# Sixty-four weight columns instead of 128 for one of five products, and another order of two

## The chip, the cores and the metric

One core of a Trainium2 chip runs the whole program. The metric is the device time of one execution in microseconds. The kernel before was timed in 3 runs.

## What is computed

The reference takes `x` of 4 x 4096 tokens with 192 channels through three layers; 16,384 tokens in all.

```
w   = softmax(weight, axis=-1)              # 8 heads x 7 taps
x1  = causal convolution of x over 7 tokens, 24 channels per head
x2  = (sigmoid(x1 @ w_gate) * (x1 @ w_val)) @ w_out      # 192 -> 1536 -> 192
out = relu(x2 @ w_in2)**2 @ w_out2                       # 192 -> 2048 -> 192
```

## The kernel before, in words

**Split numbers.** Matrix operands go to TensorE as float32r. So that a product keeps enough digits, each operand is split into a high part (the number cast to float32r) and a low part (the rest). A product is then the sum of three: high weight by high activation, high weight by low activation, low weight by high activation. The weights are split once at the start (`convert`, L126); of the hidden activations `gh` is the high part (`high`, L540, on ScalarE) and `gl` the low one (`low`, L546, on VectorE).

**Stages.** The tokens are cut into 32 tiles of 512. For each tile there is a phase of stage one (the gated layer, 12 units of 128 hidden channels) and a phase of stage two (the squared layer, 8 units of 2 x 128 hidden channels). From the sixth tile on the phases alternate: stage one of tile t, stage two of tile t - 5.

**Rows and columns.** A unit first computes its hidden channels (`rows`, L509): 9 steps, each of two matmuls. The first works on partitions 0 to 63 of the array (`HALVES[0]`), the second on 64 to 127, and each adds to a bank of its own. Then ScalarE and VectorE make `gh` and `gl` of a hidden block of 128 channels by 512 tokens (`activate`, L550). Later `cols` (L561) multiplies each block by the output weights. The 192 output channels go to two banks for each partition half: `accA` holds channels 0 to 127, `accB` channels 128 to 191. The weights for `accB` are 128 columns wide, `wb`: 64 with the high part of channels 128 to 191 and, right behind them, 64 with their low part. So one matmul with `gh` yields the high-by-high product in partitions 0 to 63 and the low-by-high product in 64 to 127. At the end of a phase `fold` (L599) adds the two halves of the array, and the upper 64 partitions of `accB` to the lower ones. A block thus takes five steps in `cols`, each again of two matmuls (L593): three for `accA` (`wa` by `gh`, `wa` by `gl`, `wl` by `gh`) and two for `accB` (`wb` by `gh`, `wb` by `gl`). A unit of stage one has one block, a unit of stage two has two.

**Order.** The program writes the order of every engine out by hand. The loop at L847 issues the rows of a unit, its activations, and then the columns of units before it (`pending`, L861 to L866); loads, convolution and stores are put between them (`side`). All matmuls of a matrix operand bring a weight load of their own, which the trace shows as LDWEIGHTS on PEld. The first matmul on a bank in a phase starts the sum anew (`start=first`), the last of a phase closes it. In the last unit of all, the order is sorted so that `accB` is finished first, and `accA` is summed over all 128 partitions in one matmul (L590).

In the first tiles the convolution runs on TensorE too, in float32 with all 128 rows (L399); later it runs on VectorE.

Of the kernel before, what the change touches and what calls it, by code (L numbers as in the profile page):

```python
# [17 lines left out]
HB = 64  # L18
# [7 lines left out]
def kernel(  # L26
# [86 lines left out]
    def weights2(u):  # L113
        if u not in w2:
            w2[u] = cp.tile([P, NW2], F32R, tag=f"u{u}", name="w2")
        return w2[u][:, 0 : 2 * NR], w2[u][:, 2 * NR :].rearrange("p (b n) -> p b n", b=2)
# [357 lines left out]
    def prep_x(t, a_on_array=False, b_on_array=False):  # L474


        p, i = divmod(t, 2)
        j = p % TPB
        sa, a = convolve("A", i, lambda: xin.pop(t), j, a_on_array)
        b = []  # L480
        if i == 0:
            pairs[p], b = convolve("B", 0, lambda: xin.pop(("B", p)), j, b_on_array)

        def over():
            done(sa)
            if i == 1:
                done(pairs.pop(p))

        return a, b, part_ops(t, x1, "x1", lambda: sa["cv"], lambda: pairs[p]["cv"], over)
# [71 lines left out]
    def cols(u):  # L561

        key = (u.kind, u.t)
        if u.f == 0:
            acc[key] = [[banks.take(f"acc{nm}") for nm in "AB"] for _ in HALVES]
        sums = acc[key]
        order = []
        for i, v in enumerate(u.hidden):  # L570
            if u.kind == 1:
                w, lo = w1[:, u.f, NR:], N1 + HB
            else:
                w, lo = weights2(u.f)[1][:, i, :], NO + HB
            wa, wb, wl = w[:, 0:P], w[:, P : 2 * P], w[:, lo : lo + P]
            first = u.f == 0 and i == 0
            order += [
                (0, wa, v.gh, first), (0, wa, v.gl, False), (0, wl, v.gh, False),
                (1, wb, v.gh, first), (1, wb, v.gl, False),
            ]  # L580
        final = u is units[-1]
        if final:

            order.sort(key=lambda step: -step[0])
        ends = {step[0]: k for k, step in enumerate(order)} if u.last else {}
        if u is units[-2]:
            shut = max(k for k, step in enumerate(order) if step[0] == 0)
        for k, (b, wt, m, first) in enumerate(order):
            if final and b == 0:
                nc.tensor.matmul(sums[0][0][1], wt, m, start=False, stop=ends[b] == k)  # L590
                continue
            for h, half in enumerate(HALVES):
                nc.tensor.matmul(  # L593
                    sums[h][b][1], wt[half], m[half], start=first,
                    stop=ends.get(b) == k or u is units[-2] and (h, b, k) == (1, 0, shut),
                )
        return u.last
# [115 lines left out]
    with tc.manual_schedule():  # L713
# [73 lines left out]
        for t in range(2, NTILE):  # L787
            at = where[1, t, 0]
            before = starts[starts.index(at) - 1]
            a, b, parting = prep_x(t)  # L790
# [56 lines left out]
        for e, u in enumerate(units):  # L847
            rows(u)
            if e < NU1:
                convert_and_activate(e, u)  # L850
            else:
                activate(u)
            for o in stores:
                o()
            stores = []
            k = e - max(s for s in starts if s <= e)

            if e >= NU1 and k == 0:
                for v in u.hidden:
                    low(v)  # L860
            due = len(pending) if k == 0 else 0 if k == 1 else len(pending) - 1  # L861
            for _ in range(due):
                v = pending.popleft()
                if cols(v):
                    stores += (evac1 if v.kind == 1 else evac2)(v.t)
            pending.append(u)  # L866
            for o in side[e]:
                o()
            if e >= NU1 and k:
                for v in u.hidden:  # L870
                    low(v)
        while pending:
            v = pending.popleft()
            if cols(v):
                for o in evac2(v.t):
                    o()
# [39 lines left out]
```

## Time and profile before

| | |
|---|---|
| median of 3 runs | 2363.5 us (2363.48 to 2364.02) |
| span of the profiled execution | 2362.0 us |
| its own time, from first to last instruction | that span; what lies around it is not in the trace |
| TensorE, matmuls | 2347.9 us busy, 20,514 of them |
| TensorE, weight loads | 2301.1 us busy, as many |
| VectorE | 1687.0 us busy (71%) |
| ScalarE | 1314.3 us busy (56%) |
| mean granted clock of TensorE | 1.000 |

PE is the matmul side of TensorE, PEld its weight loads, DVE is VectorE, ACT is ScalarE, SP the engine that starts most DMAs. "Busy" counts the time in which at least one instruction of the engine runs; matmuls overlap, so that the sum of their durations is far larger than the busy time. A row of the timeline gives start, duration, engine, line, operation, output and inputs, shape and count; a number in brackets is the idle time before it and what ended it. "64*128" in a matmul's row is rows by columns of the array that it uses.

### The profile page before, as it was taken

What the parts mean: (1) busy time and instruction counts of PE and PEld (TensorE: products, weight loads), DVE (VectorE), ACT (ScalarE), POOL (GpSimd) and SP (SyncE); (2) the same over time, 40 slices, a digit from 0 to 9 for tenths busy, and PEclk for the clock granted to TensorE, in tenths of its full rate; (3) what the DMA queues carried; (4) which work ended last, traced back from release to release, by engine and by line L of the source; (5) the groups of instructions that cost most, each with busy time, mean ns of one, the idle gap of its engine ahead of it and who ended that gap; (6) DMA issues with size and microseconds to landing.
All of it is one profiled execution on the core that took longest, in us unless ns stands there. A gap on an engine that the chain in (4) does not pass through costs nothing.

```text
span 2362.0 us, 49286 instructions
## 1 busy us (share of the span) xinstructions
PE 2347.9 (99%) x20514; PEld 2301.1 (97%) x20514; DVE 1687.0 (71%) x2679; ACT 1314.3 (56%) x2261; POOL 45.4 (2%) x98
## 2 busy tenths in 40 slices
PE   8999999999999999999999999999999999999998
PEld 5789999999999999999999999999999999999998
DVE  8787866677776776767767677676676766666776
ACT  7555655555555555545555455555555554555665
POOL 1000000000000000000000000000000000000000
PEclk9999999999999999999999999999999999999999
DMA  7123111201212111121011111111111111101111
GB/s 180 32 55 77 46 31 38 43 22 32 44 26 44 33 23 41 26 44 39 21 37 35 35 39 21 37 39 30 39 39 25 34 30 39 35 21 28 42 28 28
DMA packets 226320, 91.87 MB, mean 39 GB/s; under 512 B 202328, under 2 KB 213728, under 8 KB 226096
## 3 DMA queue, kind: packets, MB, share of 16 engines
q1 hardware_dynamic: 224608, 87.93, 17.4%
q8 instruction: 160, 2.62, 0.5%
q0 software_dynamic: 288, 0.59, 0.1%
q14 instruction: 64, 0.52, 0.1%
q10 hardware_dynamic: 1200, 0.20, 0.0%
HBM read 26.03 MB, written 12.58 MB: 16 GB/s over the span
## 4 chain that ended last, share of the span: by engine, by line
PE 82%; issue 16%; DVE 1%; ACT 1%; DMA 0%; SPq 0%; POOL 0%; POOLq 0%; DVEq 0%; ACTq 0%
PE accA L593 21%; PE ph L521 17%; PE pg L521 16%; PE pv L521 14%; PE accB L593 14%; DVE cvA L390 0%; ACT s L534 0%; DMA xiB<-in_x_dram 0%; DVE s L538 0%; ACT pair L152 0%; DMA x<-x 0%; SPq L332 0%; ACT pair L149 0%; POOL xiB L332 0%; DVE pair L174 0%
## 5 line engine op out<-in xcount | busy, mean ns | idle before, releaser
L521 PE MATMUL pg<-x,w 64*128 64x512 f32 x3456 | 842.2, 387 | 4.6 <-ACT w L181 3.6
L521 PE MATMUL pv<-x,w 64*128 64x512 f32 x3456 | 841.7, 387 | 1.0 <-DMA x<-x 0.7
L593 PE MATMUL accA<-gh,w 64*128 64x512 f32 x3576 | 842.1, 386 | 0.0
L543 ACT CAST gh<-s 128x512 fp32r<-128x512 f32 x896 | 556.8, 623 | 432.9 <-DVE s L538 426.3
L548 DVE TENSOR_TENSOR gl<-s,gh 128x512 fp32r<-128x512 f32 x896 | 599.5, 687 | 97.2 <-ACT gh L543 77.2
L521 PEld LDWEIGHTS pg<-x,w 64*128 64x128 f32 x3456 | 635.1, 184 | 18.3 <-ACT w L181 8.0
L521 PEld LDWEIGHTS pv<-x,w 64*128 64x128 f32 x3456 | 634.9, 184 | 11.8 <-DMA x<-x 1.0
L521 PE MATMUL ph<-x,w 64*128 64x512 f32 x4608 | 581.1, 386 | 0.0
L521 PEld LDWEIGHTS ph<-x,w 64*128 64x128 f32 x4608 | 535.8, 184 | 0.0
L593 PEld LDWEIGHTS accA<-gh,w 64*128 64x128 f32 x3576 | 512.7, 184 | 6.0 <-issue 2.3
L538 DVE TENSOR_TENSOR s<-pv,s 128x512 f32<-128x512 f32 x384 | 264.5, 689 | 284.2 <-ACT s L534 284.0
L538 DVE TENSOR_TENSOR s<-s 128x512 f32<-128x512 f32 x512 | 330.1, 686 | 175.9 <-ACT s L534 175.7
L593 PE MATMUL accB<-gh,w 64*128 64x512 f32 x1792 | 438.8, 386 | 0.0
L593 PE MATMUL accB<-gl,w 64*128 64x512 f32 x1792 | 438.7, 386 | 0.0
L593 PE MATMUL accA<-gl,w 64*128 64x512 f32 x1788 | 438.1, 386 | 0.0
L534 ACT ACTIVATE s<-ph 128x512 f32<-128x512 f32 x512 | 280.2, 594 | 213.4 <-PE ph L521 205.0
L534 ACT ACTIVATE s<-pg 128x512 f32<-128x512 f32 x384 | 229.1, 597 | 261.7 <-PE pg L521 202.5
L593 PEld LDWEIGHTS accB<-gh,w 64*128 64x128 f32 x1792 | 256.8, 184 | 1.9
L593 PEld LDWEIGHTS accB<-gl,w 64*128 64x128 f32 x1792 | 256.8, 184 | 1.9
L593 PEld LDWEIGHTS accA<-gl,w 64*128 64x128 f32 x1788 | 256.0, 184 | 2.0 <-DVE gl L548 0.2
L390 DVE SCALAR_TENSOR_TENSOR cvA<-xTA,cw,cvA 128x512 f32<-128x512 f32 x186 | 137.4, 739 | 0.5
L609 ACT COPY ca<-accA 128x512 f32<-128x512 f32 x64 | 37.4, 585 | 64.6 <-PE accA L593 64.6
(87 smaller groups left out, 774.4 us busy)
## 6 DMA issues: line engine op xcount, KB each, us to landing
x<-x SPq DMA_DIRECT2D x191, 256.0 KB, 3.8
out_dram<-oA SPq DMA_DIRECT2D x126, 64.0 KB, 1.9
xiA<-in_x_dram SPq DMA_DIRECT2D x124, 64.0 KB, 2.8
raw<-in_moe_w_out_dram SPq DMA_DIRECT2D x28, 192.0 KB, 3.6
out_dram<-oB SPq DMA_DIRECT2D x63, 64.0 KB, 1.9
xiB<-in_x_dram SPq DMA_DIRECT2D x60, 64.0 KB, 2.4
raw<-in_moe_w_in_dram SPq DMA_DIRECT2D x16, 192.0 KB, 3.4
raw<-in_moe_w_gate_dram SPq DMA_DIRECT2D x12, 192.0 KB, 4.0
```

The lines of the kernel that those rows point to most:

```text
L390: nc.vector.scalar_tensor_tensor(out=st["cv"], in0=st["x"][:, k : k + NT], scalar=cw[:, i, k : k + 1], in1=st["cv"], op0=ALU.mult, op1=ALU ...
L521: nc.tensor.matmul(u.banks[h][1], w[half, o + c * P : o + (c + 1) * P], xs[1][half, place[n] + p, :], start=(i == 0), stop=(i == len(steps ...
L534: nc.scalar.activation(s, u.banks[i][1], AF.Sigmoid if u.kind == 1 else AF.Relu)
L538: nc.vector.tensor_tensor(s, u.banks[1][1] if u.kind == 1 else s, s, op=ALU.mult)
L543: nc.scalar.copy(v.gh, s)
L548: nc.vector.tensor_tensor(v.gl, v.s, v.gh.bitcast(F32), op=ALU.subtract)
L593: nc.tensor.matmul(sums[h][b][1], wt[half], m[half], start=first, stop=ends.get(b) == k or u is units[-2] and (h, b, k) == (1, 0, shut),)
L609: nc.scalar.copy(ca, a1[1])
```

## The change

For the product of `wb` with `gl`, only the 64 columns with the high parts are loaded, and the output is the first 64 partitions of the bank. In every block but the first of a phase this product is issued ahead of the one with `gh`. What partitions 64 to 127 received from it, the product of the low weights with the low activations, is not computed any more. `HB` is 64.

```diff
@@ -576,8 +576,9 @@
             first = u.f == 0 and i == 0
             order += [
                 (0, wa, v.gh, first), (0, wa, v.gl, False), (0, wl, v.gh, False),
-                (1, wb, v.gh, first), (1, wb, v.gl, False),
             ]
+            upper = [(1, wb, v.gh, first), (1, wb[:, 0:HB], v.gl, False)]
+            order += upper if first else upper[::-1]
         final = u is units[-1]
         if final:
 
@@ -591,7 +592,7 @@
                 continue
             for h, half in enumerate(HALVES):
                 nc.tensor.matmul(
-                    sums[h][b][1], wt[half], m[half], start=first,
+                    sums[h][b][1][0 : wt.shape[1]], wt[half], m[half], start=first,
                     stop=ends.get(b) == k or u is units[-2] and (h, b, k) == (1, 0, shut),
                 )
         return u.last
```

## Rows read from the trace of the kernel before

**Rows 1.** The page's head: span, and busy time by engine.

```profile
span 2362.0 us, 49286 instructions
PE 2347.9 (99%) x20514; PEld 2301.1 (97%) x20514; DVE 1687.0 (71%) x2679; ACT 1314.3 (56%) x2261; POOL 45.4 (2%) x98
```

**Rows 2.** Stretches of time: length, busy time by engine, granted clock, DMA.

```profile
400.00:800.00 400.00, 400.00 (x3533) 400.00 (x3531) 282.13 (x436) 219.09 (x378) 7.68 (x16) 1.00 0.16 33
```

**Rows 3.** Chain that ended last: start, length, piece.

```profile
845.02 4.08 PE ph L521 x36
917.55 4.08 PE ph L521 x36
```

**Rows 4.** Instructions grouped by line and shape, whole span.

```profile
L593 PE MATMUL accB<-gh,w 64*128 64x512 f32 x1792 | 438.8, 386 | 0.0
L593 PE MATMUL accB<-gl,w 64*128 64x512 f32 x1792 | 438.7, 386 | 0.0
...
L593 PEld LDWEIGHTS accB<-gl,w 64*128 64x128 f32 x1792 | 256.8, 184 | 1.9
```

**Rows 5.** Timeline from 163.2 us, where a load came late.

```profile
163.32 0.58 PE L593 MATMUL accA<-gh,w 64*128 64x512 f32 x2
...
163.69 0.19 PEld L593 LDWEIGHTS accA<-gl,w 64*128 64x128 f32 x2 [0.21 <-DVE gl L548]
163.69 0.50 PE L593 MATMUL accA<-gl,w 64*128 64x512 f32 x2
163.80 0.19 PEld L593 LDWEIGHTS accA<-gh,w 64*128 64x128 f32 x2
164.03 0.40 PE L593 MATMUL accA<-gh,w 64*128 64x512 f32 x2
```

**Rows 6.** Timeline from 1003.1 us, the steady stretch.

```profile
1003.20 0.49 PE L593 MATMUL accB<-gh,w 64*128 64x512 f32 x2
1003.20 0.29 PEld L593 LDWEIGHTS accB<-gl,w 64*128 64x128 f32 x2
1003.42 0.49 PE L593 MATMUL accB<-gl,w 64*128 64x512 f32 x2
```

**Rows 7.** Timeline of PEld from 11.8 us: loads of the float32 products.

```profile
11.84 0.19 PEld L399 LDWEIGHTS cv<-xTB,diag 128*128 128x128 f32 x1 [0.24 <-issue]
12.27 0.19 PEld L399 LDWEIGHTS cv<-xTB,diag 128*128 128x128 f32 x1 [0.24 <-issue]
...
14.85 0.19 PEld L399 LDWEIGHTS cv<-xTB,diag 128*128 128x128 f32 x1 [0.24 <-issue]
```

**Rows 8.** Timeline from 19.6 us: 64 rows of the array, 128, 64 again.

```profile
19.73 0.39 PE L521 MATMUL pv<-x,w 64*128 64x512 f32 x1
...
20.05 0.30 PEld L399 LDWEIGHTS cv<-xTA,diag 128*128 128x128 f32 x2 [0.36 <-issue]
20.05 2.84 PE L399 MATMUL cv<-xTA,diag 128*128 128x512 f32 x6
...
21.88 0.19 PEld L399 LDWEIGHTS cv<-xTA,diag 128*128 128x128 f32 x1 [0.24 <-issue]
...
22.82 0.18 PEld L521 LDWEIGHTS pg<-x,w 64*128 64x128 f32 x1 [0.76 <-issue]
...
22.93 0.19 PEld L521 LDWEIGHTS pg<-x,w 64*128 64x128 f32 x1
```

**Rows 9.** Waits of PEld: who waited for whom, us in total, times, longest.

```profile
PEld accA L593 <- DVE gl L548: 0.2, 1, 0.2
```

**Rows 10.** Timeline from 30.2 us, after a pause of TensorE.

```profile
30.62 0.39 PE L593 MATMUL accA<-gl,w 64*128 64x512 f32 x2
...
32.24 0.18 PEld L521 LDWEIGHTS pg<-x,w 64*128 64x128 f32 x1
32.24 0.18 PEld L521 LDWEIGHTS pv<-x,w 64*128 64x128 f32 x1
...
32.46 0.39 PE L521 MATMUL pg<-x,w 64*128 64x512 f32 x1
32.47 0.39 PE L521 MATMUL pv<-x,w 64*128 64x512 f32 x1
```

## The prediction

> **What bounds the kernel now.** I read the page's head first: a span of 2362.0 us in which TensorE has a product running 99% of the time and a weight load 97% [rows 1]; VectorE and ScalarE are far from that. The stretches by time say that it is steady: from 400 us on there is no gap on TensorE at all, and the granted clock is 1.00 of 2.4 GHz [rows 2]. The chain shows the period: the 36 matmuls of the stage-two rows begin at 845.02 and again at 917.55 us, 72.53 us later [rows 3]. In between lie one phase of stage one and one of stage two, which by the code issue 12 x (9 + 5) + 8 x (9 + 10) = 320 steps, a step being the two matmuls of the two partition halves. So one step takes 72.53/320 = 0.2267 us, and 32 x 320 = 10,240 steps take 2321 us of the 2362. Any gain or loss of this change has to come out of the length of a step.
>
> A step can be long for two reasons, and the busy shares (99% and 97%) do not part them: its loads, or the passage of its 512 columns. The rows by shape give 184 ns to a load, whatever the tile, and 386 ns to a matmul [rows 4]; each half's loads and matmuls therefore overlap their neighbours, and a mean duration is not a cost. What parts them is a place where a load came late. At 163.69 us the loads for `accA<-gl` had waited for VectorE; their matmuls are recorded at the same moment, but run 0.50 us in place of 0.39, and the next load, which everywhere follows the start of the matmul before it, comes at 163.80 [rows 5]. So a load needs about 0.11 us before its product can pass. The following products come at 164.03, which is 0.23 after 163.80: the ordinary step, though their loads ran beside it. In the steady state the load for a product starts when the product before it does (1003.20 both) and that product comes at 1003.42 [rows 6]. A load of 0.11 us has 0.227 us to be ready in: some 0.11 us of slack on every step. **The step is the passage of the columns, and the loads lie under it.** The rows of the float32 products point the same way: their loads, 0.19 us long, stand 0.43 us apart with 0.24 idle before each [rows 7], so there too the matmul sets the pace.
>
> **The change, part by part.**
>
> 1. *The short load.* There are 384 + 2 x 256 = 896 hidden blocks, each with one step `accB<-gl`: 1792 loads and 1792 matmuls [rows 4]. Their loads go from 128 to 64 columns. The matmul still passes 512 columns, so its own time stays. A load that shrinks by half of its 0.11 us takes 0.055 us off something with 0.11 us of slack already. Cover: the passage of the product before it, 0.227 us; without that cover the gain would be 896 x 0.055 = 49 us. Taken: 0. Bounds: below, nothing lost by the load itself, as it reads less; above, what lies between a step and the bare passage of 512 columns. The nearest rows for that are the float32 products: from 11.84 to 14.85 seven of them take 3.01 us, 0.430 each [rows 7], and half of that, an estimate that takes such a product as two passes, is 0.215 us; 512 columns at one in each cycle of 2.4 GHz are 0.2133. So a step could lose 0.0117 us by the first and 0.0134 by the second; I take the second as the bound, and 896 x 0.0134 = 12.0 us.
>
> 2. *The narrower output.* The matmul writes partitions 0 to 63 of `accB` and leaves out 64 to 127. It has no row of its own in the trace: every matmul there has 128 weight columns. If the array takes it as it takes the others, 0. If not, it needs another division of the array, and the trace has the price of such a change, since the float32 products use all 128 rows and their neighbours 64. Going over: the last 64-row matmul starts at 19.73, the second float32 load, which marks the first float32 passage, at 20.05 + 0.30 - 0.19 = 20.16 us: 0.43 where a step takes 0.23, so 0.20 us lost. Coming back: the last float32 load at 21.88, so its passage at 21.88 + 0.43 = 22.31; the next 64-row passage at 22.93: 0.62 where 0.43 would do, so 0.19 us lost [rows 8]. Twice per block, 896 x 0.39 = 349 us. I take 0, because rows of the array are shared out as before (both halves of 64) and only columns would be, which no row here shows to matter.
>
> The Trainium skill speaks on both sides of this. "TensorEngine Tiling (Array Packing)", Key Properties, says that a change of tiling mode drains the engine, and lists 64x64 as a mode apart from 64x128; [rows 8] agree that a change of mode costs, about 0.2 us each. "PSUM — Partial Sum Buffer" of the Trainium skill, The four PSUM rules, says that float32r matmuls force the mask of all column groups; no run here shows that. By the first the sum would be 2712 us, by the second nothing changes.
>
> 3. *The order.* `gl` now comes ahead of `gh` on `accB`, except in the first block of a phase. Its matmuls would wait for `gl`, but `accA<-gl` stands three steps earlier in the same block and waits for the same tile: over the whole run PE's loads wait 0.2 us for `gl`, once [rows 9]. So no new wait, and nothing moves past a queue: the order of ScalarE, VectorE, POOL and SP's DMAs is untouched. The last product of a phase is still one with all 128 partitions, so the reading of `accB` starts where it did. Cost 0.
>
> 4. *The low-by-low products* that partitions 64 to 127 received are gone. They shared their columns' passage with the others, so no step goes away: 10,240 before and after. Cost 0.
>
> 5. *The last unit* keeps its order by bank; its two `accB<-gl` steps are short ones. Cost 0.
>
> Sum: 0 against the profiled span of 2362.0 us. The median of the runs, 2363.5, is 1.5 us above that span, which lies around it; so 2363.5 us.
>
> **The rivals.**
>
> *A: the loads do space the steps* by way of the remainder above the bare passage, 0.0134 us a step. For it: PEld is busy 97%, and a step is 0.2267 us and not 0.2133, a remainder that I cannot account for. Against it: the slack of 0.11 us in [rows 5], and that the step does not feel when the loads come: it is 0.23 with the two halves' loads at the same moment (32.24 to 32.47 [rows 10]) as with 0.11 between them, where two loads of 0.18 take 0.29 together [rows 6]. [...] If the remainder shrinks by half on the 896 steps, 896 x 0.0067 = 6.0 us: 2357.5; if all goes, 2351.5. Chance 0.23.
>
> *B: the array changes its division* for the 64-column product and back, at 0.39 us: 2363.5 + 349 = 2712 us. Slower already if a change cost over 0.003 us (4.7 us over 1792 changes). For it: [rows 8] on rows; against it: no row says that columns do the same. Chance 0.16.
>
> *C: the even beat is lost.* After a pause the steps are not 0.227 us at once: the products from 30.62 to 32.24 us are seven steps in 1.62 us, 0.231 each, then it settles [rows 10]. If every short load set the beat off anew, 896 x 7 x 0.0045 = 28 us: 2392. Against it: the late load of [rows 5] was followed by ordinary steps at once. Chance 0.04.
>
> *That the chip loads 128 columns anyway,* or masks them, gives the forecast's time and is part of it.
>
> **How the numbers follow.** A measurement of this kernel tells some 0.2% (4.7 us) from no change. The forecast, no change, has 0.57; A, faster, 0.23; B and C, slower, 0.20. The range takes in the forecast with 2.5 us to its upper side for what the order may do, and all of A: 2351.5 to 2366, which holds 0.80; B and C are left out.
>
> **What would show it.** Right: the chain's period stays 72.53 us; the short load's row is under 184 ns with 896 x 2 of them, its matmul still 386; the load after it starts with its matmul. A: the period falls by 0.19 to 0.38 us (28 short steps in it, 12 + 16). B: gaps before the short load and behind it, a period near 83 us. C: matmuls of 390 ns and more in the steady stretch. The forecast is wrong if the steps before or after the short load change at all.

## The result, and the profile after

The changed kernel takes 2381.28 us (2381.01 to 2381.96 in 4 runs) where the one before took 2363.76 (2363.48 to 2365.02) beside it: a ratio of 1.0073, with a 95% interval of 1.0059 to 1.0087. It is 17.5 us slower. The prediction was no change, 2363.5 us, with a range from 2351.5 to 2366.

The page's head of the changed kernel answers to [rows 1]: 18.2 us more of span, as many matmuls, and no other engine busier.

```profile
span 2380.2 us, 49089 instructions
...
PE 2366.3 (99%) x20514; PEld 2329.3 (98%) x20514; DVE 1686.8 (71%) x2679; ACT 1313.8 (55%) x2261; POOL 45.4 (2%) x98
```

The chain of the changed kernel (start, length, piece) answers to [rows 3]:

```profile
851.28 4.09 PE ph L521 x36
924.37 4.09 PE ph L521 x36
```

The period is 73.09 us and was 72.53. That is 0.56 us for the 28 short steps in it, 0.020 us each; 32 periods make 17.9 us. So the loss lies in the steady stretch and comes again in every period. Its instructions by line and shape answer to [rows 4]:

```profile
L594 PE MATMUL accB<-gl,w 64*64 64x512 f32 x1792 | 443.9, 394 | 0.0
...
L594 PE MATMUL accB<-gh,w 64*128 64x512 f32 x1792 | 436.7, 386 | 0.0
...
L594 PEld LDWEIGHTS accB<-gl,w 64*64 64x64 f32 x1792 | 207.8, 131 | 1.6
```

The change does what it says: 1792 loads take 131 ns in place of 184. But their matmuls, which pass the same 512 columns, are recorded 394 ns long in place of 386. The waits of PEld for `gl` answer to [rows 9] and have not grown, so the new order adds no wait:

```profile
PEld accA L594 <- DVE gl L548: 0.2, 1, 0.2
```

The timeline of PE in a unit of stage two of the changed kernel (start, duration, engine, line, operation, tiles, shape) shows where the 0.020 us go:

```profile
1006.10 0.49 PE L594 MATMUL accA<-gh,w 64*128 64x512 f32 x2
1006.32 0.50 PE L594 MATMUL accB<-gl,w 64*64 64x512 f32 x2
1006.56 0.49 PE L594 MATMUL accB<-gh,w 64*128 64x512 f32 x2
1006.78 0.49 PE L594 MATMUL accA<-gh,w 64*128 64x512 f32 x2
1007.02 0.49 PE L594 MATMUL accA<-gl,w 64*128 64x512 f32 x2
1007.25 0.49 PE L594 MATMUL accA<-gh,w 64*128 64x512 f32 x2
1007.47 0.50 PE L594 MATMUL accB<-gl,w 64*64 64x512 f32 x2
```

From one short product to the next, 1006.32 to 1007.47, are five steps in 1.15 us, and five settled ones would be 1.133. No single step takes the loss: they are uneven. In whole nanoseconds, from the starts of the first half's matmuls in the trace, the steps from 1006.10 on are 226, 235, 229, 232, 231, 226. The short product starts in time. The step from its start to that of the next product and the three steps behind it are too long by 8, 2, 5 and 4 ns; the fifth is as before. Over nine periods of the trace each short product loses 20 ns on the mean, in stage one, where the next one comes 14 steps on, as in stage two.

### The profile page after: what moved, and what is told of

Its sections match the earlier page's. It is cut to its first block, busy times and chain, and to the rows that moved or that the text cites. A ratio compares the mean times of both kernels' runs of the same rounds, so it can differ in the third digit from the quotient of the medians.

```text
span 2380.2 us, 49089 instructions
## 1 busy us (share of the span) xinstructions
PE 2366.3 (99%) x20514; PEld 2329.3 (98%) x20514; DVE 1686.8 (71%) x2679; ACT 1313.8 (55%) x2261; POOL 45.4 (2%) x98
## 4 chain that ended last, share of the span: by engine, by line
PE 82%; issue 16%; DVE 1%; ACT 1%; SPq 0%; DMA 0%; POOLq 0%; DVEq 0%; ACTq 0%; POOL 0%
PE accA L594 21%; PE pg L521 17%; PE ph L521 17%; PE accB L594 14%; PE pv L521 13%; PE cv L399 0%; ACT s L534 0%; SPq L332 0%; ACT pair L152 0%; DVE s L538 0%; DMA xiA<-in_x_dram 0%; DMA xiB<-in_x_dram 0%; ACT pair L149 0%; DVE pair L174 0%; DVE gl L548 0%
## 5 line engine op out<-in xcount | busy, mean ns | idle before, releaser
L594 PE MATMUL accB<-gl,w 64*64 64x512 f32 x1792 | 443.9, 394 | 0.0
L594 PEld LDWEIGHTS accB<-gl,w 64*64 64x64 f32 x1792 | 207.8, 131 | 1.6
```

What stands on the lines that cost most here:

```text
L594: nc.tensor.matmul(sums[h][b][1][0 : wt.shape[1]], wt[half], m[half], start=first, stop=ends.get(b) == k or u is units[-2] and (h, b, k) = ...
```

## The experiments

Besides the prediction's rivals, three theories were put against each other. **B, the beat**: steps with equal full loads settle at 0.2267 us, anything that shifts one of them makes the next ones uneven until they settle again, and that is the loss (the prediction's rival C, not its rival B). **D, the division** of the array: a 64-column product is taken in another way (a milder rival B). **S, the short load**: the loss grows with the shortening. Two more, the order alone (O) and a price paid within the short step itself (P), were to be ruled out.

### The order alone

Both products of `accB` with 128 columns, in the new order.

```diff
-            upper = [(1, wb, v.gh, first), (1, wb[:, 0:HB], v.gl, False)]
+            upper = [(1, wb, v.gh, first), (1, wb, v.gl, False)]
```

> The new order with full loads of 128 columns. Theory S (a load shorter than its neighbours makes its product pass late) and theory D (a product on 64 columns divides the array otherwise, and each change costs some 9 ns and an unsettled beat): as before, 2363.8 us within 1.5, period of the chain 72.53 us. Theory O (the order itself costs): 2381 us, period 73.09 us.

Measured: 2363.8 us, 1.0001 of the kernel before (0.9991 to 1.001). The chain's period is the old one:

```profile
844.76 4.08 PE ph L521 x36
917.29 4.08 PE ph L521 x36
```

72.53 us. O falls: the order costs nothing, as the prediction had it.

### The old order with short loads

The short product behind the one with `gh`, save in the last block of a phase.

```diff
-            order += upper if first else upper[::-1]
+            order += upper[::-1] if u.last and i == len(u.hidden) - 1 else upper
```

> 64 columns, but the old order (the product with the low activations behind the one with the high ones, except in the last block of a phase). S and D: 896 short steps as in the change, 2381 us within 4. O: 2363.8 us within 1.5.

Measured: 2381.7 us, 1.0076 (1.0061 to 1.0091), the changed kernel's time. The loss comes with the short product, in either order.

### Ninety-six columns

```diff
-            upper = [(1, wb, v.gh, first), (1, wb[:, 0:HB], v.gl, False)]
+            upper = [(1, wb, v.gh, first), (1, wb[:, 0:96], v.gl, False)]
```

> 96 columns loaded and written in place of 64, order as in the change; of the low-by-low products only those of 32 channels are left out. S: half of the shortening, so a loss of some 9 us, 2372 us. D: more than 64 columns take the division of 128, so no loss: 2363.8 us within 1.5.

Measured: 2395.47 us, 1.0134 (1.0117 to 1.0151). Both theories miss. The load is nearer to a full one and the product wider than 64, and the loss is nearly twice as large. The chain's period:

```profile
855.96 4.09 PE ph L521 x36
929.52 4.09 PE ph L521 x36
```

73.56 us, which is 1.03 us above the old period, or 0.037 for each of the 28. D falls in the form in which more than 64 columns are taken as 128 are, and so does S in the form in which the loss grows with the shortening. What was left was that the width itself matters, in no plain order.

### Runs of steps behind the kernel

Behind the last columns of the kernel before, steps of two matmuls were added on two free banks, of which nothing is read; the work before them is unchanged. Each of the three programs made in this way ran once, with a granted clock of 1.00 in the added steps. The list of this one has 362 steps; the 390 of its expectation are a miscount.

```diff
+        def step(n, c=0, m=NT):
+            for h, half in enumerate(HALVES):
+                nc.tensor.matmul(
+                    spare[h][c : c + n, 0:m], w[half, 0:n], x[half, 0, 0:m], start=True, stop=True
+                )
```

> The kernel before with 390 extra steps of two matmuls behind the last columns, of which nothing is read: runs of 128, 64, 72 and 32 columns by themselves, runs that alternate 128 with 64, 72 or 96, groups of two 64 among eight 128, and runs of 256 moving columns. All theories: 128 alone 0.2267 us a step. S: 64 alone 0.2267 or less; 128 with 64 and 128 with 72 both over 0.230, 128 with 96 between. D: 64 alone 0.2267; 128 with 64 over 0.230; 128 with 72 and 128 with 96 0.2267. Rival A of the prediction (the load sets the remainder above the bare passage): 64, 72 and 32 alone 0.214 to 0.220.

Measured, from the starts of the first half's matmuls (the length of a run by the number of its steps; the two rows with 256 moving columns once settled). Moving columns are the columns of activations that a matmul passes, 512 where nothing else is said:

| load columns | us a step | expected |
|---|---|---|
| 128 alone, settled | 0.2267 | 0.2267, all |
| 64 alone | 0.2303 | 0.2267 (D), that or less (S), 0.214 to 0.220 (rival A) |
| 72 alone | 0.2308 | 0.214 to 0.220 (rival A) |
| 32 alone | 0.2318 | 0.214 to 0.220 (rival A) |
| 128 and 64 in turn | 0.2316 | over 0.230 (S, D) |
| 128 and 72 in turn | 0.2300 | over 0.230 (S), 0.2267 (D) |
| 128 and 96 in turn | 0.2330 | between (S), 0.2267 (D) |
| two of 64, then eight of 128 | 0.2300 | no figure |
| 128, with 256 moving columns | 0.1200 | no figure |
| 64, with 256 moving columns | 0.1134 | no figure |

Rival A falls for 512 moving columns: a run of short loads is slower than one of full ones. Such a run does not settle to equal steps within its twenty: those of 64 alone repeat 236, 229, 224, 227, 234, 230 ns. That also goes against theory D, which had 0.2267 for them. Only the last two rows look like rival A: with 256 moving columns the remainder above the bare passage (106.7 ns, an estimate from one column in each cycle of 2.4 GHz, as in the prediction) is 13.3 ns with full loads and 6.7 with half of them.

### Single short steps, one half, and float32

The same with one step of another width among ten full ones, with a short load in one half only, with other numbers of moving columns, and with operands read as float32. Its list has 836 steps; the 730 of the expectation are a miscount.

```diff
+        def step(n0, n1, m=NT, plain=False):
+            for h, (half, n) in enumerate(zip(HALVES, (n0, n1))):
+                if n:
+                    a, c = w[half, 0:n], x[half, 0, 0:m]
+                    if plain:
+                        a, c = a.bitcast(F32), c.bitcast(F32)
+                    nc.tensor.matmul(spare[h][0:n, 0:m], a, c, start=True, stop=True)
```

> The kernel before with 730 extra steps behind the last columns, of which nothing is read: loads of 120, 112, 104, 96, 88, 80, 72, 48 and 32 columns, each as a run of 16 and as a single step among ten full ones; steps with a short load in one half only and steps of one half alone; 128 to 504 moving columns with full and with short loads; and float32 products. Theory B (the beat: steps with equal full loads settle at 0.2267 us, a load of another length shifts the moment at which its product passes, and the full steps behind it need some six steps to settle again): a single short step among ten costs 0.02 to 0.04 us, of which less than half in its own step, at any width. Theory P (the short product costs by itself, in its own step): the whole loss in its own step, none behind it. If the halves share what is disturbed, a short load in one half disturbs the other as well; if not, the other half stays at 0.2267. The float32 products, whose passage leaves the loads more time, show no loss under B, and some 0.02 us a short step under P.

Measured: one 64-column step in one half among full ones lost 20 ns, 9 of them from its own start to that of the next product and 11 in the three full steps behind that; P, with the whole loss in the step itself, falls. "At any width" was wrong: 88 columns lost nothing, and 96 some 50 ns. In runs of sixteen by themselves only 88 columns kept 0.2267; the other widths took from 0.229 (104 and 112) to 0.236 us (48) a step.

While one half ran 64-column loads in every step, with steps of 224 to 236 ns, the other half stayed at 226 to 227, so the halves did not share what was disturbed there. One stretch does not fit so simply: where one half came back behind a pause, it took nine steps of 231 to 238 ns with full loads in both halves, while the other ran at 226 to 227. What slowed it was not looked into.

A step of 256 moving columns *with full loads* left the same uneven steps that a short load leaves, with no short load near: from the first full product behind it on they are 236, 228, 233, 231 and then 226 ns. The runs with other numbers of moving columns (mean of the last eight of fourteen steps; two figures where the halves differ):

| moving columns | us a step, 128-column loads | us a step, 64-column loads |
|---|---|---|
| 128 | 0.112 | 0.060 |
| 384 | 0.174 | 0.171 and 0.177 |
| 448 | 0.207 | 0.202 |
| 480 | 0.217 | 0.217 |
| 496 | 0.223 | 0.224 |
| 504 | 0.227 | 0.229 |

So what a shorter load is worth depends on the columns that pass: it nearly halves the step at 128, gains 0.005 us at 448 and loses at 504 and 512. The 0.112 us at 128 agree with the 0.11 that the prediction took from [rows 5] as a load's need. Two things here limit theory B: equal full loads do not always settle into equal steps (with 480 columns, 221 and 212 ns take turns through all fourteen), and 504 columns settle at the 0.2267 us of 512, though fewer pass.

The float32 runs missed both ways. Matmuls of float32 by shape, first while 128 columns alone ran, then while 128 and 64 took turns (mean duration in ns behind the comma):

```profile
L900 PE MATMUL pr<-x,w 64*128 64x512 f32 x43 | 9.2, 575 | 0.0
```

```profile
L900 PE MATMUL pr<-x,w 64*128 64x512 f32 x20 | 5.6, 641 | 0.0
L900 PE MATMUL pr<-x,w 64*64 64x512 f32 x20 | 5.4, 614 | 0.0
```

In turn, one step of each took 2.065 us (from 2539.91 to 2541.98 us) where two steps of one width take 1.716 (four float32 matmuls a half at 0.429; a float32 product shows as two): 0.349 us lost on two changes of width, 0.17 each. That is near the 0.39 us for two changes by which the prediction's rival B was priced; whether the array divides itself anew there, the runs do not show. The kernel's operands are float32r, and there a 64-column step costs 0.020 us and not 0.35. Theory B had expected no loss for float32; it is another loss, and theory B says nothing of it.

### Every width from 8 to 120

```diff
+for n in range(8, 128, 8):
+    PROBES += [([(n, n)] + [F] * 16) * 2]
```

> The kernel before with 530 extra steps behind the last columns, of which nothing is read: one step with a load of 8, 16, ... 120 columns among sixteen full ones, each twice. B: every width ends in the settled step of 0.2267 us again; 88 and 120 lose less than 0.002 us, 64 and 80 some 0.020, 104 some 0.04, 96 over 0.05. Whether the free widths are a rule: if they lie 32 apart (24, 56, 88, 120), 24 and 56 lose less than 0.002 us as well; if 88 and 120 are single cases, 24 and 56 lose 0.02 like 32 and 48. If the loss grew with the shortening (S), 8 columns would lose most.

Measured: the loss of one such step is the time from the start of the full step ahead of it to that of the last of the sixteen behind it, less 17 x 226.67 ns; the two repeats agree within 1 ns.

| load columns | ns lost |
|---|---|
| 8, 88 | 0 |
| 120 | 7 |
| 40 | 14 |
| 16, 24, 32, 48, 56, 64, 80, 112 | 20 |
| 72 | 27 |
| 104 | 47 |
| 96 | 53 |

All widths end in the settled step. Where 20 ns are lost, the short product starts in time, as in the changed kernel; with 40, 72, 96, 104 and 120 columns it starts 1 to 8 ns late itself. There is no rule of 32: 24 and 56 lose 20 ns, and 120 was missed by 5. S falls for good: 8 columns lose nothing. And the loss comes in steps: each figure lies within 1 ns of a multiple of 6.67 ns (0, 1, 2, 3, 4, 7 and 8 of them). The groups by shape (mean ns behind the comma) show the short products themselves:

```profile
L893 PE MATMUL pr<-x,w 64*64 64x512 f32 x4 | 0.8, 394 | 0.0
...
L893 PE MATMUL pr<-x,w 64*104 64x512 f32 x4 | 0.8, 393 | 0.0
...
L893 PE MATMUL pr<-x,w 64*96 64x512 f32 x4 | 0.8, 388 | 0.0
...
L893 PE MATMUL pr<-x,w 64*88 64x512 f32 x4 | 0.8, 386 | 0.0
...
L893 PEld LDWEIGHTS pr<-x,w 64*104 64x104 f32 x4 | 0.3, 164 | 0.1
...
L893 PEld LDWEIGHTS pr<-x,w 64*88 64x88 f32 x4 | 0.3, 151 | 0.1
```

The load shrinks evenly with its columns, and the matmul's duration does not follow it: 386 is the duration in the settled beat, and at 88 columns the product stays in it. The duration does not rank the losses either: 96 columns, the costliest, are at 388.

### The widths in the kernel

These were the tests that could have broken B: a shorter load that must cost nothing, and one nearly full that must cost most but for 96. First 88 columns:

```diff
-            upper = [(1, wb, v.gh, first), (1, wb[:, 0:HB], v.gl, False)]
+            upper = [(1, wb, v.gh, first), (1, wb[:, 0:88], v.gl, False)]
```

> 88 columns loaded and written in place of 64, order as in the change; of the low-by-low products those of 24 channels are left in. Theory B (the beat), with the widths as the single steps among ten full ones showed them: 88 columns lost nothing there (11 steps in 0.0007 us over 11 x 0.2267), so as before, 2363.6 us within 1.5, period 72.53 us. Theory S (any shorter load costs, the more the shorter) with 64 columns at 17.5 us and 96 at 31.5: between these, 2381 to 2395 us.

Measured: 2363.74 us, 1.0001 (0.9992 to 1.001). The chain and the shapes:

```profile
846.57 4.08 PE ph L521 x36
919.10 4.08 PE ph L521 x36
```

```profile
L594 PE MATMUL accB<-gl,w 64*88 64x512 f32 x1792 | 417.2, 386 | 0.0
...
L594 PEld LDWEIGHTS accB<-gh,w 64*128 64x128 f32 x1792 | 234.5, 184 | 2.5
L594 PEld LDWEIGHTS accB<-gl,w 64*88 64x88 f32 x1792 | 204.0, 151 | 1.6
```

The 1792 loads are 33 ns shorter, the period is 72.53 us. So a shorter load and a narrower output are not dear by themselves; they cost where the even steps are lost. Then 104:

```diff
-            upper = [(1, wb, v.gh, first), (1, wb[:, 0:HB], v.gl, False)]
+            upper = [(1, wb, v.gh, first), (1, wb[:, 0:104], v.gl, False)]
```

> 104 columns in place of 64, order as in the change. B: a single such step lost 0.041 to 0.046 us among ten full ones, so 896 of them up to 37 us, less where the second short step of a stage-two unit comes before the beat has settled: 2388 to 2404 us, the slowest of all widths although its load is nearest to the full one. S: less than a fifth of a full load is saved, so less than the 17.5 us of 64 columns: 2364 to 2381 us.

Measured: 2389.65 us, 1.0109 (1.0096 to 1.0123).

```profile
853.88 4.08 PE ph L521 x36
927.24 4.08 PE ph L521 x36
```

The period is 73.36 us, 0.030 for each of the 28. Taking 24 columns off costs more than taking 64 off, as B said and S could not. "The slowest of all widths" was wrong, though: 96 is slower. Both lose less in the kernel than alone (0.030 against 0.047, 0.037 against 0.053); the second short step of a stage-two unit comes after four or five steps, and alone these widths need nine to eleven to settle. The two traces show that the missing part is there: in stage one, from one short product to the next 14 steps on, 104 columns lose 47 ns and 96 columns 53, as alone. What is left of the longer period is 17 and 24 ns for each of the sixteen in stage two.

Last, 64 columns in stage one only:

```diff
-            upper = [(1, wb, v.gh, first), (1, wb[:, 0:HB], v.gl, False)]
+            upper = [(1, wb, v.gh, first), (1, wb[:, 0:HB] if u.kind == 1 else wb, v.gl, False)]
```

> 64 columns in stage one only, where 13 full steps lie between two short ones; stage two loads 128 in the new order. B: 384 steps at 0.0197 to 0.0207 us, the loss of a single 64-column... step as of 48 and 80 columns among ten full ones: 7.7 us, 2371.3 us within 1.5. If a loss needed two short steps close together, as in stage two: 2363.6 us.

Measured: 2370.86 us, 1.0031 (1.0019 to 1.0042).

```profile
847.85 4.09 PE ph L521 x36
920.62 4.09 PE ph L521 x36
```

72.77 us: 0.24 us for 12 short steps, 0.020 each. Each short step pays by itself, and needs no second one near it.

None of these runs points to a version that is faster than the kernel before: no width that was run by itself took less than 0.2267 us a step with 512 moving columns, and the one that costs nothing gains nothing.

## Why the prediction was wrong

*What bounds the kernel* held in the main. The loss sits in the length of a step, nothing off TensorE moved, and the loads do not set the step: 33 ns less of them, at 88 columns, changed nothing. That the step is the passage of the columns and no more is too simple, as 504 columns take the same 0.2267 us.

*Part 1 failed.* "A load of 0.11 us has 0.227 us to be ready in" fits the runs, and "Taken: 0" does not follow from it; measured are some 20 ns for each of the 896 short steps, 17.5 us in all. Cover says that a load is not waited for. It does not say that a step with another load leaves the steps behind it alone. The trace of before shows only loads of 128 columns in the steady stretch, so it could not price a load of another width; the bound below, "nothing lost by the load itself, as it reads less", excluded a loss without a row. It should have been the unsettled steps of [rows 10], some 0.03 us a block.

*Rival C was what happened,* at a chance of 0.04: its sign, matmuls of 390 ns and more in the steady stretch, came (394). Its price was too high by more than half, 28 us against 17.5: it took seven uneven steps of 4.5 ns each, and measured are four, with 20 ns in all. What set its chance was a misreading: "the late load of [rows 5] was followed by ordinary steps at once". Those rows end with the first step after it. The further rows of PE in that timeline of the kernel before:

```profile
164.25 0.40 PE L593 MATMUL accB<-gh,w 64*128 64x512 f32 x2
164.49 0.40 PE L593 MATMUL accB<-gl,w 64*128 64x512 f32 x2
...
165.18 0.61 PE L521 MATMUL pg<-x,w 64*128 64x512 f32 x2
```

From 164.03 in [rows 5] to 165.18 are five steps in 1.15 us, 0.230 each: the beat was lost there too, and the matmuls' 0.40 us in place of 0.39 say so. In whole nanoseconds one half's steps are 234, 229, 232, 231, 227. With that row read, the evidence against C turns into evidence for it.

*Rival B* was priced at the cost of going over to 128 rows and back, 0.39 us. For float32r no such loss came: 64-column products lost 0.020 us. For float32 the runs showed one of 0.35. The row that the price was taken from has float32 products on one side of each change. The Trainium skill's "TensorEngine Tiling (Array Packing)", Key Properties, has a change of tiling mode drain the engine. The 0.17 us a change of the float32 runs would fit that; the 0.020 us of a float32r step show no such price.

*Rival A* fell for this kernel: with 512 moving columns no shorter load made the steps shorter; with 128, 256 and 448 it did. The Trainium skill's "Perfetto Trace Analysis", Identifying the Most-Contended Engine, takes the LDWEIGHTS busy share, beside the share of peak arithmetic, for how close TensorE is to its limit. The 97% of [rows 1] does not tell what a shorter load is worth: the 88-column run shortened 1792 loads by 18%, and the time stayed at 2363.74 us.

*Part 2* cannot be parted from part 1: each of these matmuls brings its own load, so fewer columns loaded are always fewer written, and whether the shorter load or the narrower output unsettles the steps stays open. That 88 columns cost nothing speaks against a price on narrowing as such. *Parts 3 to 5* held at 0: order alone 1.0001, no new wait, no step fewer, and with 88 columns part of the low-by-low products is left out at no cost.

*What stays open* is why a step settles at 226.67 ns and why 8 and 88 columns keep it while 80 and 96 do not. The runs show that a short step in one half leaves the other alone, that a pause, a late load, a shorter passage and most other widths lead to the same kind of uneven steps, and that the loss of a single odd step comes in multiples of 6.67 ns. They do not show what in the chip keeps that beat: the beat tells how the steps go, not why.

## What to carry to other kernels

A change to a load that hides under a passage can still cost, where a steady run of equal steps has settled into a beat: before making one instruction of such a run different, look in the trace for any place where the run was disturbed, and read on until the steps are equal again. Where one width must differ, time a few of them: here 88 columns cost nothing, 64 cost 0.020 us a step and 96 0.037. And a row that excludes a rival has to reach as far as the rival would act.

## What the runs showed of the hardware that was not expected

- Alternate widths of float32 products cost 0.17 us a change; of float32r products, at most 0.053 us for a single odd step and often 0.020.
- A lone odd step among full ones (64 rows, float32r, 512 moving columns) lost 0, 7, 14, 20, 27, 47 or 53 ns, multiples of 6.67 ns within 1, in no order of its width.
- With fewer moving columns the load's width does show: 0.1200 us a step with 128 columns and 0.1134 with 64 at 256 moving columns, 0.112 and 0.060 at 128.
- With full loads, 504 moving columns settle at the same 0.2267 us as 512, and 480 do not settle to equal steps (221 and 212 ns in turn).
- One half of the array stayed at 226 to 227 ns while the other ran unevenly at 224 to 236 with short loads.
